# Weight conversion in a fused attention and two-MLP kernel: a leaky ReLU and two bit operations for a scaled copy and three, with the table of order keys laid anew

## The chip, the cores and the metric

The program runs on one core of one Trainium2 chip. The metric is the device time of one execution, in microseconds (us): the median of several runs. The engines are named as the profile names them: PE (TensorE matmuls; PEld its weight loads), DVE (VectorE), ACT (ScalarE), POOL (GpSimd), SP (SyncE, which only issues DMAs here).

## The reference

Linear attention with exponential features, then an MLP with SiLU, then an MLP with squared ReLU. 4 batches, 8 heads, 576 positions, head size 64, 128 features; 2304 tokens, model size 512, hidden size 2048.

```python
def phi(x):
    proj = np.einsum('bhsd,df->bhsf', x, w_phi)
    proj = proj - np.max(np.abs(proj), axis=-1, keepdims=True)
    return np.concatenate([np.exp(proj), np.exp(-proj)], axis=-1)
q_p, k_p = (phi(q), phi(k))
kv = np.einsum('bhsf,bhsd->bhfd', k_p, v)
z = np.sum(k_p, axis=2)
num = np.einsum('bhsf,bhfd->bhsd', q_p, kv)
den = np.einsum('bhsf,bhf->bhs', q_p, z)[..., None] + 1e-06
x = (num / den)                       # tokens x 512
h = x @ w_in                          # first MLP
x = (h * (1.0 / (1.0 + np.exp(-h)))) @ w_out
h = np.maximum(x @ w_in2, 0.0)        # second MLP
out = (h * h) @ w_out2
```

The weights of both MLPs reach the kernel as 64-bit floating-point numbers, read as pairs of 32-bit words. The kernel itself makes 32-bit numbers of them.

## The kernel before

Products in 32 bits are made of three passes: each operand is split into a high part (a rounding copy on ACT, `hi_act`, L446) and a low part (a subtraction, `lo_on`, L450, on DVE), and high times low, low times high and high times high are summed in PSUM. In the first batch's attention the products are taken on the 32-bit numbers directly.

Attention goes by batch and by pair of heads. `keys_of(j, p)` loads keys and values, projects (L856), takes the maximum (L861), subtracts it (L867) and takes exponentials of whole 512-column blocks (L948), or, for pairs from number `bx` on, lets ACT take them from PSUM in blocks of 128 columns with the maximum as a bias (L932, after a negation, L878); then it sums keys times values (`pkv`, L964). `queries_of(b, p)` does a block of 288 positions for a pair: projection `pq` (L1051), copy to `qp` (L1058), maximum over the partitions on POOL (`qm`, L1065), subtraction (L1071), two exponentials `qe` (L1083), numerator and denominator `pn` (L1117), copy to `qn` (L1120). The denominators go over memory: SP spreads them over 96 partitions (`rr`, L1134), DVE takes the reciprocal (L1137), SP stores it (L1140) and loads it back for 64 partitions (`qb`, L1143), DVE multiplies (x, L1159), and x is split into high and low part. In these names the first number is the batch or block, the second the pair; block b has the positions 288 b to 288 b + 287 of all tokens.

The first MLP (`chunk`) goes over six stretches of tokens and 16 chunks of 128 hidden units: `h` (L1198, 12 matmuls), its SiLU in four steps on ACT and DVE, and `o` (L1237). Its first `h` needs x of all four pairs of block 0, the fourth pair for the last three of the 12 matmuls. The second MLP takes seven products instead of eight over 2 x 2 blocks: sums of weights (`ws`, `ya`: `w_adds`, L684, on POOL), `pa`, `pb`, `pc` (L1366), and `y` (L1538).

Weights are converted by `w_conv`: `mag` on ACT multiplies the upper words, read as 32-bit numbers, by a power of two (`wc`, L560), and `bits` on DVE shifts left by three and clears the sign (L565), ors three bits of the lower word in (L569), and ors the sign in (L573). There are 16 of 1024 columns for the first MLP, in the attention of the first two blocks and the early chunks, and 32 of 512 columns for the second, later. `w_split` then makes the high and low part.

The order of all instructions is made ahead of time: every step is an `Op` with a key, an engine and a cost, and `Plan.run` plays the program through, gives each engine, whenever it is free, the ready step with the lowest key, and emits the steps in that order. Each engine then works through its own queue strictly in order, and SP its DMA issues likewise. The table `KEYS` holds the numbers that set the keys (and `bx`). Where the plan leaves PE idle over 1.9 us ahead of an attention product, `idle_mm` (L1683) puts filler matmuls there, one for about each 0.43 us.

Of the kernel before, what the change touches and what calls it, by code (L numbers as in the profile page):

```python
# [8 lines left out]
F32 = mybir.dt.float32  # L9
F32R = mybir.dt.float32r  # L10
I32 = mybir.dt.int32
AF = mybir.ActivationFunctionType
ALU = mybir.AluOpType
# [64 lines left out]
class Plan:  # L78
# [16 lines left out]
    def op(self, key, engine, cost, emit, r=(), w=(), bufs=(), unit=None, after=()):  # L95
        if unit and engine == "PE":
            key -= KEYS["pe"]
        elif unit:
            key -= KEYS["ee"] if unit.early else KEYS["e1"] if unit.soon else 0
        if not unit and engine in ("ACT", "DVE"):  # L100
            key -= KEYS["el"]
        o = Op(len(self.ops), key, engine, cost, emit, unit)
        before = set(after)
        for x in r:
            before.update(self.written[x])
        for x in w:
            before.update(self.read.pop(x, ()))
            before.update(self.written.get(x, ()))
        for x in r:
            self.read.setdefault(x, []).append(o)  # L110
        for x in w:
            self.written[x] = [o]
        if unit and unit.token:
            bufs = [*bufs, unit.token]
        for b in bufs:
            if b not in self.started:
                self.started.add(b)
                b.first = o
                o.allocs.append(b)
                if b.pool in self.last:  # L120
                    self.last[b.pool][0] += 1
            else:
                before.add(b.first)
            b.users += 1
            o.frees.append(b)
        before.discard(o)
        o.waits = len(before)
        for x in before:
            x.after.append(o)
        self.ops.append(o)  # L130
        if unit:
            unit.ops.append(o)
        return o
# [142 lines left out]
def dve(n, fast=False):  # L276
    return 70 + (0.52 if fast else 1.04) * n + 60
# [6 lines left out]
def dma(kb):  # L284
    return kb
# [3 lines left out]


KEYS = {
# [6 lines left out]
}  # L298


# [1 line left out]
def attention_then_two_mlps(ctx, tc, kT, qT, v, w_phi, w1, w2, out):  # L302
    nc = tc.nc
# [66 lines left out]
    op = plan.op  # L370
# [68 lines left out]
    def get(b):  # L439
        if b.tile is None:  # L440
            b.tile = b.make()
        return b.tile
# [95 lines left out]
    def w_conv(layer, c, parts, key):  # L538

        n = f"{layer}_{c}_{parts[0]}"
        cols = 512 * len(parts)
        u = plan.unit()
        if layer == 0:
            raw = w_tile("bits", c)
            f = Buf("raw", lambda: rp.tile([128, cols], F32, tag="raw", name="wc" + n), None)
        else:
            raw = Buf("raw", lambda: rp.tile([128, 2 * cols], I32, tag="raw", name="wr" + n), None)
            f = Buf("c", lambda: cp.tile([128, cols], F32, tag="c", name="wc" + n), None)  # L550

        def load():
            src = (w1, w2)[layer][c, :, parts[0] * 512:parts[0] * 512 + cols].bitcast(I32)
            nc.sync.dma_start(out=get(raw), in_=src)

        def halves():
            return get(raw).rearrange("p (n two) -> p n two", two=2)

        def mag():
            nc.scalar.activation(out=get(f), in_=halves()[:, :, 1].bitcast(F32), func=AF.Copy, scale=2.0 ** -112)  # L560

        def bits(i):
            b, lo, hi = get(f).bitcast(I32), halves()[:, :, 0], halves()[:, :, 1]
            if i == 0:
                nc.vector.tensor_scalar(  # L565
                    out=b, in0=b, scalar1=3, scalar2=0x7FFFFFFF, op0=ALU.logical_shift_left, op1=ALU.bitwise_and
                )
            elif i == 1:
                nc.vector.scalar_tensor_tensor(  # L569
                    out=b, in0=lo, scalar=29, in1=b, op0=ALU.logical_shift_right, op1=ALU.bitwise_or  # L570
                )
            else:
                nc.vector.scalar_tensor_tensor(  # L573
                    out=b, in0=hi, scalar=-(1 << 31), in1=b, op0=ALU.bitwise_and, op1=ALU.bitwise_or
                )

        k = ("wf", layer, c, parts[0])
        hold = max([0] + [NC * i + x for i in range(NL) for x in range(NC) if key_of(i, x) <= key - 6]) if layer else 0
        r = [(("c", 0, hold // NC, hold % NC), "h")] if layer else []
        ld = op(key - P["wl"], "SP", dma(cols), load, r=r, w=[(k, 0)], bufs=[raw])  # L580
        if layer == 0:
            ld.behind = splits.get(c - NWR)
        op(key, "ACT", act(cols) + cols / 10, mag, r=[(k, 0)], w=[(k, 1)], bufs=[raw, f], unit=u)
        for i in range(3):
            op(key, "DVE", dve(cols, i < 1), lambda i=i: bits(i), r=[(k, 1 + i)], w=[(k, 2 + i) if i < 2 else k],
               bufs=[raw, f], unit=u)
        return f, u

    def w_tile(layer, c, turn=0):
        if (layer, c, turn) not in wch:  # L590
            shape, dt = [128, 4, 512], F32R
            if layer in (1, 3) and c < 2:
                wch[layer, c, turn] = Buf(
                    "wl", lambda: wide_pool().tile([128, 8, 256], F32R, tag="w", bufs=2, name=f"wl{layer}_{c}"), None
                )
                return wch[layer, c, turn]
            if layer == "bits":
                shape, dt = [128, 2048], I32
            elif layer in (1, 3):
                shape = [128, 8, 256]  # L600
            first = c // 2 in (1, 2, 4, 6) if layer in (1, 3) else c in IN_W and not turn
            wch[layer, c, turn] = Buf(
                "w" if first else "wq",
                lambda: (wp if first else late_pool()).tile(
                    shape, dt, tag="w", bufs=NC - NW if first else NWQ, name=f"w{layer}_{c}_{turn}"
                ), None
            )
        return wch[layer, c, turn]
# [1049 lines left out]
    for i, (at, cols) in enumerate(BLOCKS):  # L1658
        for q in range(NQ):
            key = base3 + (NQ * i + q * cols / 512) * fine  # L1660
# [81 lines left out]
```

## Time and profile before

| what | us |
|---|---|
| median of 3 runs (lowest, highest) | 950.94 (949.41, 952.22) |
| span of the profiled execution, first to last instruction | 947.9 |
| PE busy | 939.2 |
| DVE busy | 723.2 |
| ACT busy | 608.8 |
| POOL busy | 149.3 |

The span is what the profile shows of one execution; the time of a run has some 3 us around it. Busy times are shares of the span; an engine that is not the bottleneck may idle at no cost. In the rows further below, a bracket or a number behind "idle before" is the time that the engine stood still just before, and the arrow names what ended that wait.

### The profile page before, as it was taken

Reading aid. Unit: us, or ns where it says so; the run is one execution under the profiler, and the core shown is the slowest. Engines: PE = TensorE matmul, PEld = TensorE weight load, DVE = VectorE, ACT = ScalarE, POOL = GpSimd, SP = SyncE. Lnnn points to the kernel's source line nnn. Section 1 sums busy time; section 2 is a strip of 40 time slices with the busy share of each in tenths; the row PEclk is TensorE's granted clock in tenths of the full one; section 3 lists DMA queues with packets and bytes.
Section 4 is the critical chain, followed back from the end, with each engine's and each line's share of the span. In section 5 each row is a group of like instructions: output and inputs, shape, how many; then the busy total and the mean of one; then the engine's idle time right before and its main releaser. Section 6 shows DMA issues by size and latency. Waiting matters only on the chain.

```text
span 947.9 us, 16861 instructions
## 1 busy us (share of the span) xinstructions
PE 939.2 (99%) x6142; PEld 908.8 (96%) x6142; DVE 723.2 (76%) x1229; ACT 608.8 (64%) x1358; POOL 149.3 (16%) x128
## 2 busy tenths in 40 slices
PE   9999999999999999999999999999999999999998
PEld 8769999999999999999999999999999999999998
DVE  6999998877667778989565876777466789887951
ACT  7989868888877787777334554666565665544431
POOL 3230013200022000321000333341101330000000
PEclk9999999999999999999999999999999999999999
DMA  8758634553324555667768775456336784543421
GB/s 325 251 195 278 224 147 153 175 161 107 121 77 134 191 180 188 207 181 228 232 230 288 256 272 179 160 206 205 116 130 233 226 290 142 156 149 119 145 81 66
DMA packets 83613, 175.44 MB, mean 185 GB/s; under 512 B 15050, under 2 KB 44874, under 8 KB 76874
## 3 DMA queue, kind: packets, MB, share of 16 engines
q1 hardware_dynamic: 83386, 174.23, 55.6%
q8 instruction: 48, 0.79, 0.3%
q14 instruction: 35, 0.29, 0.1%
q10 hardware_dynamic: 144, 0.13, 0.0%
HBM read 125.67 MB, written 48.59 MB: 184 GB/s over the span
## 4 chain that ended last, share of the span: by engine, by line
PE 92%; DVE 2%; ACT 1%; DMA 0%; issue 0%; POOL 0%; DVEq 0%; ACTq 0%
PE h L1198 21%; PE o L1237 21%; PE y L1538 19%; PE pb L1366 8%; PE pa L1366 5%; PE pc L1366 5%; PE pn L1117 4%; PE pkv L918 3%; PE pk L856 2%; PE pkv L964 2%; PE pq L1054 1%; PE pq L1055 1%; DVE w L450 0%; DVE x L1159 0%; ACT kp L932 0%; DVE qp L1071 0%
## 5 line engine op out<-in xcount | busy, mean ns | idle before, releaser
L1237 PE MATMUL o<-gh,w 128*128 128x432 f32 (+1 forms) x768 | 217.4, 340 | 0.0
L1198 PE MATMUL h<-x,w 128*128 128x432 f32 (+1 forms) x1152 | 216.1, 337 | 0.3 <-DVE w L450 0.3
L1198 PEld LDWEIGHTS h<-x,w 128*128 128x128 f32 x1152 | 195.9, 188 | 6.8 <-DVE w L450 0.5
L1237 PEld LDWEIGHTS o<-gh,w 128*128 128x128 f32 x768 | 139.9, 188 | 3.8
L1237 PE MATMUL o<-gl,w 128*128 128x432 f32 (+1 forms) x384 | 129.6, 338 | 0.0
L1065 POOL PARTITION_ALL_REDUCE qm<-qp x32 | 74.0, 2334 | 226.0 <-ACT qp L1058 212.4
L1202 ACT ACTIVATE a<-h 128x432 f32<-128x432 f32 (+1 forms) x96 | 47.4, 493 | 69.2 <-PE h L1198 69.0
L1206 DVE SCALAR_TENSOR_TENSOR a<-a,h 128x432 f32<-128x432 f32 (+1 forms) x96 | 52.8, 550 | 41.0 <-ACT a L1202 40.5
L1237 PEld LDWEIGHTS o<-gl,w 128*128 128x128 f32 x384 | 72.2, 188 | 1.9
L684 POOL TENSOR_TENSOR ws<-ws 128x256 f32<-128x256 f32 x52 | 45.8, 883 | 142.9 <-DVE w L450 108.4
L450 DVE TENSOR_TENSOR gl<-a,gh 128x432 fp32r<-128x432 f32 (+1 forms) x96 | 55.0, 572 | 15.3 <-ACT gh L446 14.5
L446 ACT CAST gh<-a 128x432 fp32r<-128x432 f32 (+1 forms) x96 | 49.9, 520 | 25.3 <-DVE a L1206 24.7
L890 ACT ACTIVATE ke<-pk,mx 112x128 f32<-112x128 f32 (+1 forms) x160 | 44.5, 374 | 0.0
L1083 ACT ACTIVATE qe<-qp 128x576 f32<-128x576 f32 x64 | 41.7, 682 | 4.2 <-DVE qp L1071 3.7
L1538 PE MATMUL y<-yb,w 128*128 128x256 f32 x316 | 44.0, 278 | 0.0
L450 DVE TENSOR_TENSOR qo<-qe,qh 128x576 fp32r<-128x576 f32 x48 | 38.7, 820 | 5.7 <-ACT qh L446 5.0
L1117 PE MATMUL pn<-qh,kv 128*65 128x288 f32 x192 | 42.9, 294 | 0.0
L1538 PEld LDWEIGHTS y<-yb,w 128*128 128x128 f32 x316 | 40.1, 188 | 0.0
L1381 DVE TENSOR_TENSOR glq<-pb,aq 128x384 f32<-128x384 f32 x24 | 13.3, 555 | 34.3 <-PE pb L1366 34.3
L964 PEld LDWEIGHTS pkv<-v,kp 112*128 112x128 f32 (+1 forms) x320 | 36.6, 192 | 0.3
L1159 DVE TENSOR_TENSOR x<-qn,qb 64x288 f32<-64x288 f32 x64 | 31.5, 492 | 7.1 <-DMA qb<-rd 6.6
L964 PE MATMUL pkv<-v,kp 112*128 112x128 f32 (+1 forms) x320 | 36.9, 275 | 0.0
(405 smaller groups left out, 2471.6 us busy)
## 6 DMA issues: line engine op xcount, KB each, us to landing
w<-w1d SPq DMA_DIRECT2D x30, 1024.0 KB, 5.3
wbits<-w SPq DMA_DIRECT2D x16, 1024.0 KB, 7.2
wr<-w SPq DMA_DIRECT2D x32, 512.0 KB, 5.3
fold<-gd SPq DMA_DIRECT2D x32, 512.0 KB, 3.7
w2d<-wc SPq DMA_DIRECT2D x32, 256.0 KB, 4.3
qr<-qT SPq DMA_DIRECT2D x56, 144.0 KB, 4.2
ws<-w2d SPq DMA_DIRECT2D x26, 256.0 KB, 4.0
w1d<-w SPq DMA_DIRECT2D x6, 1024.0 KB, 4.9
```

The source lines that it names most:

```text
L446: nc.scalar.copy(out=dst, in_=src)
L450: e.tensor_tensor(out=dst, in0=src, in1=hi.bitcast(F32), op=ALU.subtract)
L684: nc.gpsimd.tensor_tensor(out=get(f)[:, o], in0=get(f)[:, a], in1=get(f)[:, b], op=how)
L964: nc.tensor.matmul(get(ps)[:, o:o + 128], get(kps[2 * g + s])[:nt, 2 * i + a], get(vt)[:nt, c:c + 128], start=t == 0 and a == 0 and s == 0 ...
L1065: nc.gpsimd.partition_all_reduce(get(mx), get(pr).rearrange("p a t -> p (a t)"), 128, bass.bass_isa.ReduceOp.absmax)
L1117: nc.tensor.matmul(get(ps)[:D1, :HB], w, get(e)[:, t], start=x == 0, stop=x == len(ops) - 1)
L1198: nc.tensor.matmul(get(ps)[:, :cols], a, x[:, cc, :cols], start=k == 0, stop=k == 3 * ND - 1)
L1202: nc.scalar.activation(out=get(gb)[0][:, :cols], in_=get(ps)[:, :cols], func=AF.Tanh, scale=0.5)
L1206: nc.vector.scalar_tensor_tensor(out=a, in0=a, scalar=1.0, in1=get(ps)[:, :cols], op0=ALU.add, op1=ALU.mult)
L1237: nc.tensor.matmul(get(acc)[:, :cols], a, g[:, :cols], start=c == 0 and x == 0, stop=c == NC - 1 and x == 2)
L1366: nc.tensor.matmul(get(ps)[:, :QB], ws[a][:, f], row(b, y, cc), start=first and k == 0, stop=k == 5, skip_group_check=True,)
L1538: nc.tensor.matmul(get(acc)[:, d * 256:d * 256 + half], get(ws[a][0])[:, ws[a][1], s], both(y)[:, j], start=q == 0 and d == 0 and x == 0, ...
```

## The change

`mag` becomes a leaky ReLU (`Prelu`) with a scale of 2^16 and a slope of 2^-32 for negative numbers, so that the sign stays in place when the result is shifted left by three. The operation that set the sign, and the mask in the first one, go. So there are two bit operations for each conversion and not three. `Plan` is told of one step less. Nearly all numbers of `KEYS` change, `bx` from 3 to 4: the fourth pair of batch 0 takes its exponentials by 512 columns as well.

```diff
 KEYS = {
-    "k0s": 15.74, "q0s": 15.35, "q0": 6.0, "w0": 71.12, "ws": 0.43, "we": -9.35, "Q1": 57.33, "A1": -5.43,
+    "k0s": 17.1, "q0s": 15.35, "q0": 6.0, "w0": 71.19, "ws": 1.46, "we": -8.93, "Q1": 56.24, "A1": -4.91, "Q2":
...
         def mag():
-            nc.scalar.activation(out=get(f), in_=halves()[:, :, 1].bitcast(F32), func=AF.Copy, scale=2.0 ** -112)
+            nc.scalar.activation(
+                out=get(f), in_=halves()[:, :, 1].bitcast(F32), func=AF.Prelu, scale=2.0 ** 16, alpha=2.0 ** -32
+            )
 
         def bits(i):
-            b, lo, hi = get(f).bitcast(I32), halves()[:, :, 0], halves()[:, :, 1]
+            b = get(f).bitcast(I32)
             if i == 0:
-                nc.vector.tensor_scalar(
-                    out=b, in0=b, scalar1=3, scalar2=0x7FFFFFFF, op0=ALU.logical_shift_left, op1=ALU.bitwise_and
-                )
-            elif i == 1:
-                nc.vector.scalar_tensor_tensor(
-                    out=b, in0=lo, scalar=29, in1=b, op0=ALU.logical_shift_right, op1=ALU.bitwise_or
-                )
+                nc.vector.tensor_scalar(out=b, in0=b, scalar1=3, scalar2=None, op0=ALU.logical_shift_left)
             else:
                 nc.vector.scalar_tensor_tensor(
-                    out=b, in0=hi, scalar=-(1 << 31), in1=b, op0=ALU.bitwise_and, op1=ALU.bitwise_or
+                    out=b, in0=halves()[:, :, 0], scalar=29, in1=b, op0=ALU.logical_shift_right, op1=ALU.bitwise_or
                 )
...
-        for i in range(3):
-            op(key, "DVE", dve(cols, i < 1), lambda i=i: bits(i), r=[(k, 1 + i)], w=[(k, 2 + i) if i < 2 else k],
+        for i in range(2):
+            op(key, "DVE", dve(cols, i < 1), lambda i=i: bits(i), r=[(k, 1 + i)], w=[(k, 2) if i < 1 else k],
                bufs=[raw, f], unit=u)
```

The lines behind the diff stand four lower in the new file (L450 is the same line, L1159 becomes L1155). What the new numbers move is seen in the built order.

**SP ahead of the first h.** The DMA issues around the load of `qb0_3`, the reciprocals of block 0's fourth pair. Before:

```order
L1134 DMA rr0_3_592<-qn0_3_577 96x1x6
L1143 DMA qb0_2_612<-rd_98 64x576
L1140 DMA rd_98<-rr0_3_592 96x6
L1143 DMA qb0_3_651<-rd_98 64x576
L1134 DMA rr1_0_658<-qn1_0_640 96x1x6
L1134 DMA rr1_1_670<-qn1_1_660 96x1x6
L633 DMA w1d_96<-w0_4_0_642 128x2048
```

Now:

```order
L1130 DMA rr0_3_590<-qn0_3_575 96x1x6
L1139 DMA qb0_2_607<-rd_98 64x576
L1136 DMA rd_98<-rr0_3_590 96x6
L1130 DMA rr1_0_635<-qn1_0_623 96x1x6
L1130 DMA rr1_1_656<-qn1_1_645 96x1x6
L1139 DMA qb0_3_664<-rd_98 64x576
L629 DMA w1d_96<-w0_4_0_567 128x2048
```

The load of `qb0_3` has moved behind the two spreads of block 1's denominators.

**DVE at the same place**, up to the product x0_3 and what follows. `qp1` is the subtraction for block 1, `wc0` a conversion and `w0` a low part of the first MLP's weights. Before:

```order
L1137 RECIPROCAL rr0_3_592<-rr0_3_592 96x6
L573 SCALAR_TENSOR_TENSOR wc0_4_0_493<-wbits_4_0_371,wc0_4_0_493 128x1024
L1159 TENSOR_TENSOR x0_2_647<-qn0_2_501,qb0_2_612 64x288 x2
L1071 TENSOR_TENSOR qp1_2_596<-qp1_2_596,qm1_2_614 128x576
L1071 TENSOR_TENSOR qp1_3_607<-qp1_3_607,qm1_3_632 128x576
L450 TENSOR_TENSOR x_0_588<-x0_2_647,x_0_588 128x288
L450 TENSOR_TENSOR w0_4_0_642<-wc0_4_0_493,w0_4_0_642 128x2x512
L569 SCALAR_TENSOR_TENSOR wc0_5_0_547<-wbits_5_0_443,wc0_5_0_547 128x1024
L1159 TENSOR_TENSOR x0_3_688<-qn0_3_577,qb0_3_651 64x288 x2
L1137 RECIPROCAL rr1_0_658<-rr1_0_658 96x6
L573 SCALAR_TENSOR_TENSOR wc0_5_0_547<-wbits_5_0_443,wc0_5_0_547 128x1024
L450 TENSOR_TENSOR x_0_588<-x0_3_688,x_0_588 128x288
```

Now (the subtraction `qp1_2` and then the reciprocal `rr0_3` stand just ahead of these rows):

```order
L1067 TENSOR_TENSOR qp1_3_596<-qp1_3_596,qm1_3_605 128x576
L1155 TENSOR_TENSOR x0_2_637<-qn0_2_499,qb0_2_607 64x288 x2
L450 TENSOR_TENSOR w0_4_0_567<-wc0_4_0_451,w0_4_0_567 128x2x512
L450 TENSOR_TENSOR x_0_558<-x0_2_637,x_0_558 128x288
L450 TENSOR_TENSOR w0_5_0_577<-wc0_5_0_523,w0_5_0_577 128x2x512
L567 TENSOR_SCALAR wc0_6_0_538<-wc0_6_0_538 128x1024
L1133 RECIPROCAL rr1_0_635<-rr1_0_635 96x6
L569 SCALAR_TENSOR_TENSOR wc0_6_0_538<-wbits_6_0_472,wc0_6_0_538 128x1024
L1155 TENSOR_TENSOR x0_3_684<-qn0_3_575,qb0_3_664 64x288 x2
L1133 RECIPROCAL rr1_1_656<-rr1_1_656 96x6
L567 TENSOR_SCALAR wc0_7_0_669<-wc0_7_0_669 128x1024
L450 TENSOR_TENSOR x_0_558<-x0_3_684,x_0_558 128x288
```

The last bit operations on `wc0_4` and `wc0_5` are gone, and the low part of `w0_5` and work on `wc0_6` and `wc0_7` have moved ahead of the low part of x0_3; the reciprocal `rr0_3` has moved behind `qp1_2`.

**ACT around the copies to `qp1`**, which POOL's maxima of block 1 wait for. `qe0_3` are the last exponentials of block 0's queries, `wc0` conversions (L560), `w0` high parts, `kv0_3` the copy of keys times values, `qn` the copies of numerators and denominators. Before:

```order
L1083 ACTIVATE qe0_3_1_544<-qp0_3_481 128x576
L560 ACTIVATE wc0_5_0_547<-wbits_5_0_443 128x1024
L975 COPY kv0_3_554<-pkv0_3_503 128x260
L1058 COPY qp1_0_556<-pq1_0_0_549 128x288
L1058 COPY qp1_0_556<-pq1_0_1_552 128x288
L1058 COPY qp1_1_567<-pq1_1_0_558 128x288
L560 ACTIVATE wc0_6_0_569<-wbits_6_0_527 128x1024
L1120 ACTIVATE qn0_3_577<-pn0_3_0_562,eps_105 65x288
L1120 ACTIVATE qn0_3_577<-pn0_3_1_571,eps_105 65x288
L446 CAST x_0_588<-x0_0_574 128x288
L1058 COPY qp1_1_567<-pq1_1_1_579 128x288
```

Now (the first copy to `qp1_0` stands ahead of these rows):

```order
L1079 ACTIVATE qe0_3_1_535<-qp0_3_464 128x576
L560 ACTIVATE wc0_6_0_538<-wbits_6_0_472 128x1024
L1054 COPY qp1_0_479<-pq1_0_1_540 128x288
L971 COPY kv0_3_550<-pkv0_3_501 128x260
L1054 COPY qp1_1_554<-pq1_1_0_542 128x288
L446 CAST x_0_558<-x0_0_544 128x288
L1054 COPY qp1_1_554<-pq1_1_1_548 128x288
L1054 COPY qp1_2_564<-pq1_2_0_556 128x288
L446 CAST w0_4_0_567<-wc0_4_0_451 128x2x512
L1116 ACTIVATE qn0_3_575<-pn0_3_0_561,eps_105 65x288
L446 CAST w0_5_0_577<-wc0_5_0_523 128x2x512
L1054 COPY qp1_2_564<-pq1_2_1_579 128x288
```

The copies to `qp1_0` have moved ahead of `kv0_3`, and the high parts of `w0_4` and `w0_5` have moved ahead of the last copy to `qp1_2`.

Elsewhere: PE's filler rows ahead of the first h go from eight matmuls (16 passes, as a 32-bit product has two) at three places to two matmuls at one; the first 63 rows of PE and its last 2067 are the same; on ACT one conversion, one high part and one copy have moved ahead of the last copy to `qp0_3`. At the start of the second MLP DVE's low parts of the last `ws` and the first `ghq` stand in the same succession as before.

## Rows read from the trace of the kernel before

**Rows 1.** The page: busy us (share of the span) xinstructions; busy tenths.

```profile
PE 939.2 (99%) x6142; PEld 908.8 (96%) x6142; DVE 723.2 (76%) x1229; ACT 608.8 (64%) x1358; POOL 149.3 (16%) x128
```

**Rows 2.** Timeline, PE: start, us, engine, line, out<-in, count, idle before.

```profile
51.32 4.18 PE L1117 MATMUL pn<-qe,kv 128*65 128x288 f32 x16 [1.26 <-ACT qe L1083]
...
57.01 0.70 PE L1117 MATMUL pn<-qe,kv 128*65 128x288 f32 x2 [0.64 <-ACT qe L1083]
57.97 3.61 PE L1117 MATMUL pn<-qe,kv 128*65 128x288 f32 x14 [0.26 <-ACT qe L1083]
61.20 3.55 PE L1198 MATMUL h<-x,w 128*128 128x288 f32 x24
```

**Rows 3.** Timeline around the start of the second MLP, DVE, POOL and PE.

```profile
596.18 2.51 DVE L450 TENSOR_TENSOR w<-ws,w 128x256 fp32r<-128x256 f32 x4
...
596.73 3.36 POOL L684 TENSOR_TENSOR ws<-ws 128x256 f32<-128x256 f32 x4 [14.14 <-ACT g_0gh L1415]
...
599.21 0.44 PE L1366 MATMUL pb<-xt_5h,w 128*128 128x384 f32 x1 [0.93 <-DVE ghq L1381]
```

**Rows 4.** Groups by line and form, 24 to 62 us: busy us, mean ns.

```profile
L1683 PE MATMUL pn<-wbl 128*128 128x256 f32 x16 | 3.9, 379 | 0.0
```

**Rows 5.** Stretches: us, busy PE PEld DVE ACT POOL, PEclk, DMA share, GB/s.

```profile
50.00:55.00 5.00, 3.74 (x16) 2.04 (x16) 4.99 (x6) 3.90 (x7) 5.00 (x2) 1.00 0.10 27
```

**Rows 6.** Timeline, POOL, ahead of the first h.

```profile
44.39 2.65 POOL L1065 PARTITION_ALL_REDUCE qm<-qp  x1 [4.15 <-ACT qp L1058]
47.83 7.63 POOL L1065 PARTITION_ALL_REDUCE qm<-qp  x3 [0.78 <-ACT qp L1058]
```

**Rows 7.** Timeline, DVE, ahead of the first h.

```profile
52.18 0.18 DVE L1137 RECIPROCAL rr<-rr 96x6 f32<-96x6 f32 x1
...
55.42 1.43 DVE L1071 TENSOR_TENSOR qp<-qp,qm 128x576 f32<-128x576 f32 x2
...
57.13 1.22 DVE L450 TENSOR_TENSOR w<-wc,w 128x1024 fp32r<-128x1024 f32 x1
58.27 1.22 DVE L569 SCALAR_TENSOR_TENSOR wc<-wbits,wc 128x1024 int32<-128x1024 int32 x1
59.41 0.91 DVE L1159 TENSOR_TENSOR x<-qn,qb 64x288 f32<-64x288 f32 x2
...
61.55 0.45 DVE L450 TENSOR_TENSOR x<-x,x 128x288 fp32r<-128x288 f32 x1
...
62.02 1.25 DVE L565 TENSOR_SCALAR wc<-wc 128x1024 int32<-128x1024 int32 x2
```

**Rows 8.** Timeline, ACT, ahead of the first h.

```profile
31.51 2.17 ACT L932 ACTIVATE kp<-pk,mx 112x128 f32<-112x128 f32 x8
...
38.54 2.04 ACT L446 CAST w<-wc 128x1024 fp32r<-128x1024 f32 x2
41.13 1.26 ACT L1083 ACTIVATE qe<-qp 128x576 f32<-128x576 f32 x2 [0.55 <-DVE qp L1071]
42.30 1.15 ACT L560 ACTIVATE wc<-wbits 128x1024 f32<-128x1024 f32 x1
...
43.60 1.00 ACT L1058 COPY qp<-pq 128x288 f32<-128x288 f32 x3
...
57.24 1.81 ACT L1083 ACTIVATE qe<-qp 128x576 f32<-128x576 f32 x3
```

**Rows 9.** Timeline, SP's DMA issues, ahead of the first h.

```profile
53.83 0.44 SPq L1143 DMA_DIRECT2D qb<-rd  x1
55.36 2.55 SPq L1134 DMA_DIRECT2D rr<-qn  x2
```

**Rows 10.** Tile qb, 20 to 80 us: from issue to landing.

```profile
DMA to landing us min/median/max: 2.8/4.7/7.9
```

**Rows 11.** Groups by line and form: busy us, mean ns, idle before.

```profile
L573 DVE SCALAR_TENSOR_TENSOR wc<-wr,wc 128x512 int32<-128x512 int32 x32 | 21.9, 684 | 0.3
...
L573 DVE SCALAR_TENSOR_TENSOR wc<-wbits,wc 128x1024 int32<-128x1024 int32 x16 | 19.2, 1212 | 0.1
...
L948 ACT ACTIVATE kp<-kd 112x512 f32<-112x512 f32 x12 | 6.8, 633 | 4.5 <-DVE kd L867 4.5
```

10 rows, old and new, of the table KEYS are left out of this document.

## Prediction

> **What bounds the kernel now.** I read the page's busy times first: TensorE (PE) is busy 939.2 of 947.9 us, 99% of the span and in the tenths of every slice but the last, VectorE (DVE) 723.2, ScalarE (ACT) 608.8 [rows 1]. So PE bounds the kernel, and time can go only where PE stands still or works for nothing. The timeline of PE shows where that is. From the first matmul of the MLP, h at 61.20 [rows 2], it runs on, but for one longer wait of 0.93 us at 599.21 [rows 3]. Ahead of 61.20, in the attention of the first batch, it waits for `qe` before 51.32, 57.01 and 57.97, for 1.26, 0.64 and 0.26 us [rows 2], and runs 3.9 us of filler matmuls (L1683), 16 passes whose result is thrown away [rows 4]. Between 50 and 55 PE is busy 3.74 us of 5 and DVE 4.99 [rows 5]: there DVE is the full engine. The most that the early part can give back is fillers and waits, 3.9 + 2.2 = 6.1 us, 0.6% of the time.
>
> Two chains end at h. The first: the last of POOL's maxima ends at 47.83 + 7.63 = 55.46 [rows 6], DVE subtracts it (55.42 to 56.85 with its neighbour [rows 7]), ACT takes the exponentials (the last three end at 59.05 [rows 8]), PE multiplies until 61.20: 5.7 us from POOL's end to h. The second: the reciprocal `rr` of the fourth pair at 52.18 [rows 7], its store, the load of `qb` at 53.83 [rows 9], the product x at 59.41, its low part from 61.55 to 62.00 [rows 7]. That feeds the last quarter of h_0's 12 matmuls. The 24 matmuls of h_0 and h_1 take 3.55 us [rows 2], some 0.13 from start to start, so the eleventh is due at 62.5 and h_0 is through by 62.8. Both chains are within half a microsecond of deciding; shortening one alone gives little.
>
> **What is removed.** Sixteen bit operations of 1024 columns, 1.21 us each, and 32 of 512 columns, 0.68 us each [rows 11]: 19.2 + 21.9 = 41.1 us of DVE. Nearly all of it lies beside a full PE, which hides it, so it gives nothing by itself. Six of the sixteen stand ahead of the low part of x: 6 x 1.14 = 6.8 us of DVE (1.14 from start to start, as at 57.13, 58.27, 59.41 [rows 7]). The shift that loses its second scalar stays one instruction over the same data; I cost it as before, 0.62 (1.25 for two [rows 7]). The trace has no leaky ReLU. The nearest row is the exponential, 0.63 us for 512 columns [rows 11], against 1.15 for a conversion's 1024 [rows 8]: by columns they are alike, so I take no difference, with -0.1 and +0.1 us each as bounds, on an engine that is not the bound. The built program holds one table load, as before, so no switch of tables is added.
>
> **The first chain.** The fourth pair's keys go from narrow exponentials (eight take 2.17 us [rows 8], 20 some 5.4, with three negations 6.0) to four wide ones of 0.63 [rows 11] and two of half the width, some 3.3, and three DVE subtractions (512, 512 and 256 columns, by the 1.21 for 1024 some 0.6, 0.6, 0.3). That frees 2.7 us of ACT, but a conversion (1.15), a weight's high part (half of the 2.04 for two [rows 8]) and one copy (0.3), 2.5 us, now stand ahead of that pair's last copy. I take no shift. Behind `qe` (41.13 to 42.30) ACT now runs one conversion, 1.15, and then the copy, 0.3, that POOL's next maximum wants; before, `kv` and another copy were ahead of it. 42.30 + 1.15 + 0.3 = 43.7 against 44.3 (43.60 and two of three copies in 1.00 us [rows 8]): 0.6 us sooner, so POOL starts at 43.8 instead of 44.39. Its four maxima take 2.65 + 7.63 = 10.3 us [rows 6]. The 0.8 us that it waited between 47.04 and 47.83 can go, but the copy for the third now stands behind a weight's high part on ACT that waits for DVE, 0 to 1.2 us. With 0.4 of that POOL ends at 54.5 instead of 55.46 (54.1 to 55.3), and PE could start h at 60.2 instead of 61.20 (59.8 to 61.0).
>
> **The second chain.** Two things move against it. On DVE the `rr` of the fourth pair now stands behind the third subtraction, which needs POOL's third maximum; I put it near 54 instead of 52.18. On SP the load of `qb` now stands behind two spreads of the next block's denominators, which wait for ACT. Before, those two were issued from 55.36 to 57.91 [rows 9]; with the first chain some 0.7 us sooner the load goes out near 57.2 instead of 53.83. With the 2.8 us that such a load took at best [rows 10] it lands at 60.0. DVE has by then, from the fourth subtraction at 54.5: 0.72 (half of 1.43) + product 0.91 + weight 1.14 + x low part 0.45 + weight 1.14 + shift 0.62 + reciprocal 0.18 + or 1.14 = 6.3 [rows 7], so it turns to the product at 60.8 (before 59.41), and the load is not waited for. Then 0.91, a reciprocal 0.18 and a shift 0.62, and the low part (0.45) ends at 63.0, against 62.00. So although six operations are gone, those that are pulled ahead (a weight's low part, the shift and or of one weight, the shift of another) and the later `rr` fill their place. With the eleventh and twelfth matmul behind it h_0 is through near 63.2. The first chain alone would have it through 1.6 us after h starts, 60.2 + 1.6 = 61.8. My second sum counts the short operations at their full duration, not from start to start, and POOL at its middle, so it may be up to a microsecond long; I take 62.5 between the two, **-0.3 us** for the early part against 62.8, with bounds -1.5 (DVE's queue is short, the first chain decides and gains what it can) and +1.5 (every wait above at its upper end).
>
> **Later.** Between 62 and 590 us PE has no idle group of note before, and DVE only gets lighter. At 596.18 four low parts of weights on DVE take 2.51 us beside four POOL additions (from 596.73), and PE waits 0.93 us for the sum that stands behind them [rows 3]. In the new order DVE and POOL run the same operations there in the same succession, so I leave that wait in place: **0**, bounds -0.9 (DVE arrives early enough to have them done) and 0. PE's last 2067 rows are the same as before, the end too. New waits between 62 and 590: **0**, bounds 0 and +1.5.
>
> **Sum.** 947.9 - 0.3 + 0 + 0 = 947.6 us of span. The median of the runs is 3.0 us above the span of before, so 950.6 us (before 950.94). What a measurement of this kernel can tell from no change is about 0.3%, 2.9 us: faster is under 948.1, slower over 953.8.
>
> **Rivals.**
>
> (a) PE's early waits go: DVE, relieved of 6.8 us, comes to x in time and the first chain is shorter than my sum, so that h_0 is through 2.9 to 5 us sooner. For it: the fillers shrink from three places to one, 16 passes to 4, and their number follows what the planner expects PE to idle. Against: the queue of SP and the operations pulled ahead on DVE. With 3.5 us it is 950.94 - 3.5 = 947.4. Chance 0.22.
>
> (b) Slower: the load of `qb` on SP. It now waits for ACT's copies of the next block's denominators, and what stands behind it on SP waits too. If it lands 7.9 us after its issue, the longest of its kind [rows 10], x starts at 57.2 + 7.9 = 65.1 instead of 60.8, h_0 is through 2.4 us later (0.91 + 0.18 + 0.62 + 0.45 + 0.26), at 67.5 against 62.8, and the time is 950.94 + 4.7 = 955.6. Slower by 2.9 us it is when h_0 is through at 65.7, x begins at 63.3, and the landing takes 6.1 us. Against it: the median of such a landing is 4.7 [rows 10], and the DMA engines were busy a tenth of the time in 50 to 55 us [rows 5]. Chance 0.07.
>
> (c) The clock. In 50 to 55 us, with PE busy 3.74 of 5, the granted clock was 1.00, which is 2.4 GHz [rows 5]. With 4 filler passes PE does less there. If it were granted 1.2 GHz from there to h, 24 passes of `pn`, 0.26 us each (14 in 3.61 [rows 2]), would take 6.2 us more: 950.6 + 6.2 = 956.8 at most, as some is hidden behind the wait for x. The trace shows no fall at waits of up to 1.26 us and has no longer ones. Chance 0.05. The Trainium skill, page "TensorE: Matmul & The Clock Gate", section "HAM oscillation — how this bites in real kernels", says that gaps in which PE idles bring the clock back to half rate; by it the fillers would be worth their time and the sum would be that of this rival, by the row it is that of the forecast.
>
> (d) The new order of the middle (keys and queries of the later batches, the second layer's weights) costs PE 3 to 4 us of new waits: 953.6 to 954.6. Against it: DVE loses work there. Chance 0.05.
>
> The forecast, h_0 through within 1.5 us of 62.5 and no more than 1.5 us of new waits behind it, has chance 0.61.
>
> **How the numbers follow.** Forecast 950.6. Its own bounds are 950.6 - 1.5 - 0.9 = 948.2 and 950.6 + 1.5 + 1.5 = 953.6; (a) reaches below, (b) to (d) above. To leave out no more than 2 in 10 the range goes to 946.8, which holds most of (a), and to 954.0. Faster by over 0.3%: (a), 0.22. Slower: (b), (c) and a little of (d), 0.13. Within: 0.65.
>
> **What would show it.** Right: DVE some 40 us less busy and PE's span all but the same; h's first matmul sooner than 61.2, but a pause within the first twelve until x's low part ends near 63; `qb` of the fourth pair issued near 57; the wait for `ghq` near 599 still there. Wrong: x's low part before 61 (then (a)), `qb` landing after 63 (b), a granted clock under 1.00 before h (c), PE waits between 62 and 590 (d), or conversions on ACT that take over 1.3 us.

## The result and the profile after

The changed kernel took 959.06 us (median; 958.54 to 960.83), beside 951.13 for the kernel before: a ratio of 1.009, interval 1.0074 to 1.0107. It is 0.9% slower, 8 us. The prediction was 950.6, within 946.8 to 954.0; the time lies 5 us above that range.

The page's busy times of the changed kernel, as in [rows 1]; its span is 957.1 us, 9.2 more than before. (In the runs that are listed with their spans, a run's time lies 1.7 to 2.1 us above its span, not 3. So the 947.9 of before belongs to an execution some 1.3 us faster than the median, and the difference of the spans is that much more than the difference of the medians.)

```profile
PE 940.5 (98%) x6130; PEld 907.2 (95%) x6130; DVE 688.0 (72%) x1184; ACT 607.2 (63%) x1341; POOL 150.8 (16%) x128
```

VectorE (DVE) has 35.2 us less to do. TensorE (PE) is as busy as before, and the span grew all the same: PE stands still more. The view of waits says where; its columns are who waited for whom, us in sum, times, and the longest. PE from 62 to 940 us, the kernel before:

```profile
PE pb L1366 <- DVE ghq L1381: 0.9, 1, 0.9
PE h L1198 <- DVE w L450: 0.3, 1, 0.3
```

The changed kernel:

```profile
PE pb L1362 <- DVE glq L1377: 3.1, 1, 3.1
PE pq L1050 <- DVE ql L450: 1.7, 2, 1.2
PE h L1194 <- ACT x L446: 0.7, 1, 0.7
PE o L1233 <- ACT gh L446: 0.6, 1, 0.6
PE o L1233 <- DVE gl L450: 0.4, 2, 0.2
PE pq L1050 <- ACT qn L1116: 0.4, 1, 0.4
PE pb L1362 <- DVE ghq L1377: 0.4, 1, 0.4
```

Two kinds of wait have become ten, of which seven are shown. The same can be counted from PE's starts: the distance from one matmul's start to the next, less the regular distance for its shape (0.12 us for 256 columns, 0.13 for 288, 0.17 for 384, 0.20 for 432), summed over a stretch. In this table "before" has its stretches at the same work, where that lies some us earlier.

| stretch of the changed kernel, us | lost before | lost now | difference |
|---|---|---|---|
| start of h (61.20 before, 60.57 now) | | | -0.63 |
| from h to 70, without the keys' products | 0.40 | 2.32 | +1.92 |
| 70 to 160 | 4.64 | 5.07 | +0.43 |
| 160 to 210 | 0.08 | 1.84 | +1.76 |
| 210 to 400 | 0.59 | 0.54 | -0.05 |
| 400 to 445 | 0 | 3.45 | +3.45 |
| 590 to 612 | 1.29 | 0.65 | -0.63 |
| 612 to 640 | 0 | 3.35 | +3.35 |
| behind 640 | 0.46 | 0.06 | -0.41 |

The differences add up to the 9.2 us of span. (Of what is lost between 70 and 160 in both kernels, some 2 us lie in the keys' products, part of which stand further apart than the regular distance.) The early part cost 1.3 us net. The rest is 7.9 net: three places that the prediction had put at nought make up 8.6, and small gains take some of it back.

The table sets one execution against one. Three runs further below stand in the order of the changed kernel up to 330 us at least (the old pace, `xs` on VectorE, stores reckoned late). In them h starts at 59.50, 60.27 and 59.55, the early part costs 0.2, 0.8 and 0.3 us net, and the stretch from 160 to 210 loses 1.44, 0.08 and 1.16. So the first rows, and place 3 below, hold to about a microsecond.

**Place 1, 612 us.** DVE, POOL and PE in the changed kernel, from the timeline (start, us, engine, line, operation, count, idle before and what ended it):

```profile
612.05 6.60 DVE L450 TENSOR_TENSOR w<-ws,w 128x256 fp32r<-128x256 f32 x4
618.58 0.54 DVE L1377 TENSOR_TENSOR glq<-pb,aq 128x384 f32<-128x384 f32 x1
...
609.61 4.83 POOL L1314 TENSOR_TENSOR xs<-xr 128x768 f32<-128x768 f32 x2
614.41 3.96 POOL L1314 TENSOR_TENSOR xs<-xr,xs 128x768 f32<-128x768 f32 x2
...
619.18 0.44 PE L1362 MATMUL pb<-xt_3h,w 128*128 128x384 f32 x1 [3.09 <-DVE glq L1377]
```

The kernel before, the same four low parts, and the same four additions on POOL:

```profile
606.44 1.41 DVE L450 TENSOR_TENSOR w<-ws,w 128x256 fp32r<-128x256 f32 x4
...
630.75 3.98 POOL L1318 TENSOR_TENSOR xs<-xr 128x768 f32<-128x768 f32 x2
634.70 4.57 POOL L1318 TENSOR_TENSOR xs<-xr,xs 128x768 f32<-128x768 f32 x2
```

Four low parts that took 1.41 us take 6.60 when POOL's wide additions (`xs`) run beside them, and the sum `glq` that PE waits for stands behind them. Before, `xs` began 24 us behind these four low parts: in POOL's queue it stood behind the sums `ya5` and `ya7`, which had to wait for DVE. In the new order these two come ahead of the last `ws`, so nothing holds `xs` back.

**Place 2, 416 to 440 us.** ACT's queue, from the timeline of the changed kernel:

```profile
416.31 0.66 ACT L560 ACTIVATE wc<-wr 128x512 f32<-128x512 f32 x1 [3.58 <-DMA w2d<-wc]
...
430.78 0.67 ACT L560 ACTIVATE wc<-wr 128x512 f32<-128x512 f32 x1 [5.19 <-DMA w2d<-wc]
...
433.12 0.54 ACT L446 CAST gh<-a 128x432 fp32r<-128x432 f32 x1
```

ACT stands at a conversion that needs a buffer, and the buffer is free only when the store of the weights before the last has landed. Behind the conversion on ACT wait the SiLU and the high part `gh`, and PE waits for that at 433.72. Over the whole program, the group of these conversions (busy us, mean ns, idle before it and what ended that), before and now:

```profile
L560 ACT ACTIVATE wc<-wr 128x512 f32<-128x512 f32 x32 | 21.4, 674 | 10.2 <-DMA wr<-w 8.2 <-DMA w2d<-wc 1.1 <-DMA ws<-w2d 0.9
```

```profile
L560 ACT ACTIVATE wc<-wr 128x512 f32<-128x512 f32 x32 | 21.5, 673 | 24.8 <-DMA w2d<-wc 23.5 <-DMA wr<-w 1.1
```

23.5 us of waiting for stores in place of 1.1. Two keys stand behind this: `w2a` 66.15 to 66.29 and `w2b`, the step from one conversion to the next, 1.8 to 0.72. The 32 conversions now lie between 333 and 487 us; before they lay between 336 and 567. There are two buffers, and a store takes 5.8 us in the median from issue to landing. The leaky ReLU itself costs nothing: 673 ns against 674.

**Place 3, 166 us.** DVE in the changed kernel:

```profile
159.36 1.92 DVE L1155 TENSOR_TENSOR x<-qn,qb 64x288 f32<-64x288 f32 x2 [1.34 <-DMA qb<-rd]
161.31 0.19 DVE L1133 RECIPROCAL rr<-rr 96x6 f32<-96x6 f32 x1
...
165.12 0.91 DVE L1155 TENSOR_TENSOR x<-qn,qb 64x288 f32<-64x288 f32 x2 [1.49 <-DMA qb<-rd]
166.07 0.76 DVE L450 TENSOR_TENSOR ql<-qr,ql 64x576 fp32r<-64x576 f32 x1
```

A product x that takes 0.91 us took 1.92, since POOL's maximum began at 159.40. So the reciprocal behind it, its store and its load came a microsecond later, DVE stood 1.49 us for that load, and `ql`, which PE needs, stood behind.

### The profile page after: what moved, and what is told of

Read it like the earlier page. It is cut to its first block, busy times and chain, and to the rows that moved or that the text cites. A ratio compares the mean times of both kernels' runs of the same rounds, so it can differ in the third digit from the quotient of the medians.

```text
span 957.1 us, 16766 instructions
## 1 busy us (share of the span) xinstructions
PE 940.5 (98%) x6130; PEld 907.2 (95%) x6130; DVE 688.0 (72%) x1184; ACT 607.2 (63%) x1341; POOL 150.8 (16%) x128
## 4 chain that ended last, share of the span: by engine, by line
PE 83%; DMA 6%; DVE 6%; ACT 3%; issue 1%; POOL 1%; SPq 0%; DVEq 0%; ACTq 0%
PE y L1534 19%; PE o L1233 18%; PE h L1194 17%; PE pb L1362 7%; PE pc L1362 5%; PE pa L1362 5%; PE pk L852 3%; PE pkv L914 3%; PE pkv L960 3%; DMA w2d<-wc 2%; PE pn L1113 2%; DMA wbits<-w 2%; DVE w L450 1%; DMA qb<-rd 1%; DVE x L1155 1%
## 5 line engine op out<-in xcount | busy, mean ns | idle before, releaser
L450 DVE TENSOR_TENSOR gl<-a,gh 128x432 fp32r<-128x432 f32 (+1 forms) x96 | 62.4, 650 | 20.4 <-ACT gh L446 19.9
L680 POOL TENSOR_TENSOR ws<-ws 128x256 f32<-128x256 f32 x52 | 49.3, 950 | 158.9 <-DVE w L450 110.0
L1155 DVE TENSOR_TENSOR x<-qn,qb 64x288 f32<-64x288 f32 x64 | 33.5, 523 | 13.2 <-DMA qb<-rd 12.7
L450 DVE TENSOR_TENSOR w<-ws,w 128x256 fp32r<-128x256 f32 (+2 forms) x39 | 34.3, 907 | 11.3 <-ACT w L446 7.4
L450 DVE TENSOR_TENSOR qo<-qe,qh 128x576 fp32r<-128x576 f32 x48 | 35.1, 750 | 6.2 <-ACT qh L446 3.4
L560 ACT ACTIVATE wc<-wr 128x512 f32<-128x512 f32 x32 | 21.5, 673 | 24.8 <-DMA w2d<-wc 23.5
```

The costliest lines, as they stand in the source:

```text
L450: e.tensor_tensor(out=dst, in0=src, in1=hi.bitcast(F32), op=ALU.subtract)
L680: nc.gpsimd.tensor_tensor(out=get(f)[:, o], in0=get(f)[:, a], in1=get(f)[:, b], op=how)
```

## What the experiments showed

Three theories stood at the start. A, **the pace**: the time is lost through the keys `w2a` and `w2b`, at places 1 and 2. B, **the operations**: the new conversion itself costs it. C, **the early part**: fillers and the load of `qb` ahead of h. Where an experiment changes a key or an operation, the plan is played anew and other instructions move too, unless the text says otherwise.

**The new conversion with all keys of before.** All 32 numbers that the change sets go back, among them

```diff
-    "w2a": 66.29, "w2b": 0.72, "bx": 4,
+    "w2a": 66.15, "w2b": 1.8, "bx": 3,
```

> The changed kernel with every key of the table as before (bx = 3 too): the leaky ReLU and the two bit operations alone. Theory A (the pace): the 8 us come from one key, the step from one conversion of the second MLP's weights to the next (w2b, 1.8 before, 0.72 now), so this kernel is within 2 us of before, 949 to 953, with under 0.5 us of PE's waits between 400 and 450 us and no wait over 1.2 us near 600 to 620. Theory B (the operations): the conversion itself costs the time, by a slower ScalarE instruction or by what a lighter VectorE triggers: 957 to 960.

965.24 us, ratio 1.0151 (1.0137 to 1.0164). Neither theory said that much. With the old pace the conversions no longer wait for stores; their idle time is all for loads:

```profile
L560 ACT ACTIVATE wc<-wr 128x512 f32<-128x512 f32 x32 | 21.6, 675 | 13.3 <-DMA wr<-w 13.3
```

But ahead of h PE stands 4.48 us at once for `qe`, after which the granted clock is 0.50 from 52 to 56 us; and between 400 and 450 PE loses some 7 us where theory A had left under 0.5: there ACT stands in line 3.68 us for a load of weights and 2.88 for a load of queries. So the stores behaved as theory A said, and its time failed: old numbers played with one operation less are a new order too, and a bad one.

**The old conversion with all new keys.** The same 32 numbers, set in the kernel before:

```diff
-    "w2a": 66.15, "w2b": 1.8, "bx": 3,
+    "w2a": 66.29, "w2b": 0.72, "bx": 4,
```

> The kernel before, with three bit operations and the scaled copy, and the new table of keys (bx = 4 too). Theory A (the pace): as slow as the changed kernel or slower, 957 to 962, since a converted buffer is held by one operation more; ScalarE waits over 15 us in sum for the stores of converted weights (1.1 us before). Theory B (the operations): 949 to 953.

969.08 us, ratio 1.0192 (1.0176 to 1.0209). Slow as A said, and slower than its 957 to 962. ACT waits for the stores, as it said:

```profile
L560 ACT ACTIVATE wc<-wr 128x512 f32<-128x512 f32 x32 | 21.3, 669 | 29.1 <-DMA w2d<-wc 29.0
```

Yet only some 5 of the 18 us are lost between 400 and 450; the rest goes in many waits of up to 1.7 us elsewhere. These two runs cannot price the conversion. They show that neither half of the change stands by itself: a table of keys is made for one set of operations.

**The changed kernel with the old pace.**

```diff
-    "w2a": 66.29, "w2b": 0.72,
+    "w2a": 66.15, "w2b": 1.8,
```

> The changed kernel with the two keys of the second MLP's weights (start w2a and step w2b) as before, all others new. In its order POOL's sums ya5 and ya7 stand behind the last ws again. Theory A (the pace): both the waits between 416 and 440 us (3.4 us) and the one at 619 us (3.3 us) go: 959.1 - 6.7 = 952.4, between 951.3 and 954. Theory B (the operations) or a cause ahead of 62 us (the load of qb): 957 to 960.

953.34 us, ratio 1.0027 (1.0016 to 1.0038): 5.7 us of the loss are gone with two keys. ACT no longer waits for stores, `xs` stands behind `ya5` and `ya7` again, and the four low parts take 1.42 us:

```profile
609.05 1.42 DVE L450 TENSOR_TENSOR w<-ws,w 128x256 fp32r<-128x256 f32 x4
...
633.37 3.98 POOL L1314 TENSOR_TENSOR xs<-xr 128x768 f32<-128x768 f32 x2
```

It is at the upper end of what A said, since 1.2 us of waits are left between 400 and 450 (PE stands 0.81 for `gl` at 446).

**Place 1 alone: POOL's wide additions on VectorE.**

```diff
-            e = "DVE" if s == 0 else "POOL"
+            e = "DVE"
```

> The changed kernel with the eight additions of 768 columns for the later blocks of the second MLP (xs, L1314) on VectorE and not on POOL, all keys new. If POOL's four additions beside VectorE's low parts are what makes four of them take 6.6 us at 612 us, these take about 1.4 us again and PE's wait of 3.25 us at 619 goes: 959.1 - 3.2 = 955.9 (955 to 957). If the low parts are slow for another reason, or VectorE is late there anyway, the wait stays or moves: 958 to 960.

953.95 us, ratio 1.0038 (1.0025 to 1.0051). All of the program up to 590 us stands in the order of the changed kernel. DVE at the place:

```profile
609.16 1.42 DVE L450 TENSOR_TENSOR w<-ws,w 128x256 fp32r<-128x256 f32 x4
611.17 0.56 DVE L1377 TENSOR_TENSOR glq<-pb,aq 128x384 f32<-128x384 f32 x1 [0.59 <-PE pb L1362]
```

Now DVE waits for PE and not PE for DVE: the wait of 3.1 us is gone, and POOL beside DVE was its cause. The gain, 5.1 us, is more than the 3.2 expected. The profiled execution shows where the rest may lie, in unchanged order: the stretch of place 3 loses 0.08 us and not 1.84, and place 2 some 0.8 less. At place 3 the product came 0.75 us sooner, ahead of POOL's maximum at 159.15:

```profile
158.61 0.92 DVE L1155 TENSOR_TENSOR x<-qn,qb 64x288 f32<-64x288 f32 x2 [0.84 <-DMA qb<-rd]
```

0.92 us, and PE did not wait at 165. So what place 3 costs hangs on a few tenths of a microsecond; that POOL's maximum is its cause is read from these two traces, and no run moves it alone.

**Place 2 alone: the plan is told when stores land.**

```diff
-        op(key, "SP", dma(256), store, r=[k], w=[(k, "d")], bufs=[f], unit=u)
+        op(key, "SP", dma(256), store, r=[k], w=[(k, "d")], bufs=[f], unit=u).late = 3500
```

> The changed kernel with all its keys, but the plan reckons 3.5 us more until a stored half of converted weights has landed (the plan puts 3.0 us, the trace shows 5.8 in the median, up to 9.6), so that it starts fewer conversions whose buffer isn't free yet. If ScalarE's wait in line for these stores is what starves TensorE between 416 and 440 us, ScalarE's waits for them fall from 23.5 us to under 8 and TensorE's waits between 400 and 450 from 3.45 to under 1.5. POOL's sums ya5 and ya7 stand behind the last ws in its order, so the wait at 619 goes too: 952 to 954. If the waits of 416 to 440 come from VectorE or from loads, they stay: 955 to 957.

953.60 us, ratio 1.0033 (1.0022 to 1.0044), with the new pace of 0.72 kept. The conversions' waits:

```profile
L560 ACT ACTIVATE wc<-wr 128x512 f32<-128x512 f32 x32 | 21.4, 673 | 1.8 <-DMA wr<-w 1.7
```

No wait for a store is left, PE loses 1.1 us between 400 and 450 where it lost 3.45, and place 1 is gone with it, by the order. That is the cause below the key: the plan reckons that a store has landed 3.0 us after its issue, the chip takes 5.8, and ACT pays the difference in line.

**The new pace alone, in the kernel before.**

```diff
-    "w2a": 66.15, "w2b": 1.8,
+    "w2a": 66.29, "w2b": 0.72,
```

> The kernel before, three bit operations and its own keys, with the start and step of the second MLP's weights alone as in the changed kernel (w2a 66.29, w2b 0.72). The pace theory: ScalarE waits over 15 us for the stores (1.1 before) and TensorE 2 to 8 us between 350 and 500 us: 953 to 960. ya5 and ya7 stay behind the last ws, so there is no wait over 1.5 us between 600 and 640. If the pace only harms together with the new operations or the other keys: 949.5 to 952.

956.36 us, ratio 1.0062 (1.0047 to 1.0077). ACT waits 29.6 us for stores and PE loses 5.1 us between 400 and 450 (none before), with three bit operations and old keys otherwise. So place 2 needs neither the new conversion nor the rest of the table.

**The early part: the reciprocal and x of block 0 first**, on top of the old pace.

```diff
-        op(key, "SP", dma(3), spread, r=[(Q, "num", 0), (Q, "num", 1)], w=[(Q, "r0")], bufs=[num, rr], unit=u).late = 1500
+        op(key, "SP", dma(3), spread, r=[(Q, "num", 0), (Q, "num", 1)], w=[(Q, "r0")], bufs=[num, rr], unit=u).late = 1500 if b else 0
...
-        op(key, "DVE", 2 * dve(HB), mul, r=[(Q, "r3"), (Q, "num", 0), (Q, "num", 1), *ahead], w=[(Q, "x")],
+        op(key - 40 * (b == 0), "DVE", 2 * dve(HB), mul, r=[(Q, "r3"), (Q, "num", 0), (Q, "num", 1), *ahead], w=[(Q, "x")],
```

> As the run with w2a and w2b of before (953.3), and in block 0 the plan reckons no extra 1.5 us for a spread of denominators and puts the product x first: the reciprocal rr0_3 stands ahead of VectorE's subtraction qp1_2, the load of qb0_3 ahead of the second spread of block 1, and fewer weight operations ahead of x's low part. If the second chain (rr, qb, x's low part) is what holds the first h, its waits between 61 and 70 us (2.0 us, before 0.4) fall under 0.8 and the time to 951 to 952.3. If the first chain or something else holds it, 952.8 to 954.

968.46 us, ratio 1.0189 (1.0164 to 1.0214). h_0 and h_1 run without a pause, 0.4 us lost from h to 70 as before, but hardly because x came sooner: its low part starts at 61.91, against 62.19 in the run with the old pace, on which this one builds. h itself starts at 61.57 and not at 59.50 as there, and the product behind h_1 at 64.97 and not at 64.63. So this run doesn't show which chain holds the first h; that the second one does (rr, `qb`, x) rests on PE's two waits for x in the trace of the changed kernel, shown in the next section. And a few instructions moved ahead of h played out into another program behind: no fillers at all ahead of h, and waits of 2.7 us for x at 245 and 3.9 for `gh` at 455. The forecast of the whole from one place failed, as mine had.

**The conversion alone, order kept.** Here the plan goes on reckoning with a third bit operation that issues nothing, so that all engines' instructions stand as before and only DVE's third operation is gone. In the kernel before, the leaky ReLU takes the place of the copy, the shift loses its mask, and

```diff
-            else:
-                nc.vector.scalar_tensor_tensor(
-                    out=b, in0=hi, scalar=-(1 << 31), in1=b, op0=ALU.bitwise_and, op1=ALU.bitwise_or
-                )
```

> The leaky ReLU and the two bit operations in the order of the kernel before: the plan still reckons with a third bit operation, which issues nothing, so every engine's instructions stand as before and VectorE's third bit operation is gone. This is the conversion alone, which the run with the old keys was not, since the plan was played anew there. If the order costs the time and the conversion nothing: 948.5 to 951.5, TensorE's waits as before (1.3 us near 599, none over 0.6 elsewhere behind 62 us), ScalarE's conversions 0.67 and 1.15 to 1.19 us each. If the conversion costs by itself: over 953.

949.58 us, ratio 0.9989 (0.9980 to 0.9999) to the kernel before: 0.6 us faster by the medians, with an interval that ends just short of 1: the one version here that beats both kernels. PE ahead of h:

```profile
57.49 3.61 PE L1117 MATMUL pn<-qe,kv 128*65 128x288 f32 x14 [0.26 <-ACT qe L1083]
60.72 3.55 PE L1198 MATMUL h<-x,w 128*128 128x288 f32 x24
```

h starts 0.48 us sooner than in [rows 2] and runs through. That is of the size of the gain, but one execution can't show that it is the gain: in the run with the new pace alone, whose order is that of the kernel before up to 360 us, h starts at 61.97, 0.77 later than in [rows 2]. 34.9 us of DVE less are worth half a microsecond or so, since PE covers the rest. Theory B is out.

**The order alone, conversion undone.** The old conversion in the order of the changed kernel: the third bit operation follows the second at once, and nothing else moves. In the changed kernel the copy takes the place of the leaky ReLU, the shift has its mask again, and the second step is

```diff
+            for x, n, o in ((lo, 29, ALU.logical_shift_right), (hi, -(1 << 31), ALU.bitwise_and)):
+                nc.vector.scalar_tensor_tensor(out=b, in0=x, scalar=n, in1=b, op0=o, op1=ALU.bitwise_or)
```

> The scaled copy and three bit operations in the order of the changed kernel: the second bit operation is followed at once by the third, all other instructions stand as in the changed kernel. If the order costs the time, this one is as slow as the changed kernel or slower (its buffers are held 0.7 us longer each): 958 to 964, with the waits near 420 to 440 and 619 us. If the conversion costs the time: 950 to 953.

975.92 us, ratio 1.0276 (1.0259 to 1.0293), more than I had thought. The waits for stores (20.3 us) and the one at place 1 are there:

```profile
627.08 6.61 DVE L450 TENSOR_TENSOR w<-ws,w 128x256 fp32r<-128x256 f32 x4
...
634.21 0.69 PE L1362 MATMUL pb<-xt_3h,w 128*128 128x384 f32 x1 [3.10 <-DVE glq L1377]
```

With the runs that keep an order, the four corners are:

| | order of before | new order |
|---|---|---|
| scaled copy, three bit operations | 950 to 951 | 975.9 |
| leaky ReLU, two bit operations | 949.6 | 959.1 |

The conversion gains 0.6 us in the old order and 17 in the new one, which leans on it. The largest part of the 17, 5.8 us, lies ahead of h: with the old conversion DVE is busy 5.82 of 6 us from 44 to 50 (4.86 in the changed kernel), PE stands 3.16 us ahead of 47.34 and 3.46 ahead of 56.65, the granted clock is 0.50 behind each (48 to 50 and 58 to 60 us), and h starts at 66.40 and not at 60.57. The order costs 9.5 us where the conversion is the new one.

**The fillers**, taken out of the run with the order kept. All 16 passes go, 12 of them between 48 and 56 us and four near 35.

```diff
-                    idle_mm(o.allocs[0], int((o.start - end - 900) / 430))
+                    pass
```

> The run with the conversion in the order of before (949.6), without the filler matmuls (12 passes, in stretches that end before h). Everything else stands as there. If the fillers only take up time in which TensorE waits anyway, the time stays at 949 to 950.5 and the granted clock at 1.00 up to h. If they keep the clock: a wait of about 3.1 us (1.24 and the 1.9 of the fillers) ahead of the products pn near 51 us is followed by a granted clock under 1.00, up to 16 passes of 0.13 us more each, and the time is 950.5 to 953.

950.08 us, ratio 0.9995 (0.9985 to 1.0005), some 0.5 us over the run with them; the intervals overlap. In the trace the effect is plain. PE, and the stretches (us, busy of PE, PEld, DVE, ACT and POOL, granted clock, DMA share, GB/s):

```profile
51.66 5.60 PE L1117 MATMUL pn<-qe,kv 128*65 128x288 f32 x16 [2.99 <-ACT qe L1083]
```

```profile
50.00:52.00 2.00, 0.34 (x1) 0.29 (x2) 2.00 (x3) 1.07 (x2) 2.00 (x2) 0.83 0.27 74
52.00:54.00 2.00, 2.00 (x5) 0.91 (x4) 1.99 (x4) 1.49 (x4) 2.00 (x2) 0.50 0.03 1
```

After a wait of 2.99 us the granted clock is 0.50, that is 1.2 GHz, and sixteen products take 5.60 us that took 4.18 [rows 2]. h starts at 61.70, 0.98 us later than with fillers; 0.41 of that was there ahead of the place already (the products of `pn` at 44.09 in place of 43.68), so the 12 passes may be worth some 0.6 us of the 1.42, and the rest hides in the waits for `qe` that follow. Executions of one order differ in h's start by as much, so this price is not shown.

## Why the prediction was wrong

**What bounds the kernel:** right. PE's standing still is all that changed the time; 35 us of DVE did not.

**What is removed:** right. The conversions on ACT cost what they did, and the run with the order kept puts the gain at 0.6 us. (DVE is 35.2 us less busy, not 41.1: operations overlap their neighbours, 1.22 long and 1.14 from start to start, and 1.75 came in with three more subtractions of the keys.)

**The first chain:** close in its end, by luck in part, since its terms were off in both directions. POOL began 1.1 us later than the sum had it (44.91 for 43.8): ACT stood for a load at the conversion ahead of the copy, a wait that the sum had at nothing. Its four maxima took 9.24 us, without any gap, for 10.3 and a gap of 0.4; they ended at 54.15 (54.5). From there to h it took 6.4 us (5.7), and h started at 60.57 (60.2).

```profile
43.40 1.13 ACT L560 ACTIVATE wc<-wbits 128x1024 f32<-128x1024 f32 x1 [1.15 <-DMA wbits<-w]
...
44.91 9.24 POOL L1061 PARTITION_ALL_REDUCE qm<-qp  x4 [4.90 <-ACT qp L1054]
```

**The second chain:** the working was right, the choice behind it was not. The load of `qb` was issued at 58.28 (57.2), the product started at 61.35 (60.8), and the low part started at 62.97 and ended at 63.4 (63.0). PE shows the pause within the first h, 0.75 us for the high part of x, which the sum did not have, and 0.19 for the low part:

```profile
60.57 1.56 PE L1194 MATMUL h<-x,w 128*128 128x288 f32 x9
62.89 0.40 PE L1194 MATMUL h<-x,w 128*128 128x288 f32 x1 [0.75 <-ACT x L446]
63.47 2.10 PE L1194 MATMUL h<-x,w 128*128 128x288 f32 x14 [0.19 <-DVE x L450]
```

I then took 62.5 as a middle between this chain and the first, where the later of the two decides. The sum alone (63.2) would have said +0.4. With h's start, the net up to 70 us was 1.3 against the -0.3 forecast, inside the bound of 1.5.

**Later, near 599:** right as far as it went: the wait for `ghq` is still there, 0.38 in place of 0.93. But I looked at that place alone. POOL's `xs` came forward onto the next four low parts, 10 us on. The rows of POOL's order show it: with `ya5` and `ya7` ahead of the last `ws`, the next in its queue is `xs`. The bound was 0; it was +3.35. So this term failed as well.

**New waits between 62 and 590: 0, bounds 0 and +1.5.** This is the step that failed first. It measured 5.6 us (1.8 at 160 to 210, 3.45 at 400 to 445, some tenths ahead of them). Rival (d) named 3 to 4 us of new waits, and got 0.05, because "DVE loses work there". At place 2 DVE's load had no part in it: the wait came from ACT, which stands in line for a buffer that a store holds. At place 3 DVE came late in spite of less work, behind a product slowed beside POOL's maximum and a load. I had read how closely the second layer's conversions now follow each other only as DVE's relief, and had not asked which resource sets how fast they may follow: two buffers and the landing of a store.

**Rivals:** (a) did not come, (b) neither: the load of `qb` was issued at 58.28, and DVE went from its queue to the product at 61.35 without waiting. (c) did not come in the changed kernel: the granted clock stayed at 1.00 up to h with 4 filler passes. In the runs where PE stood 2.7 us and more there it fell, so 0.05 was low for its kind, but not for this kernel.

## What to carry to other kernels

A change that speeds an engine nobody waits for gains little (0.6 us here), while a new order played out for it can cost far more (9.5 us). So keep the order fixed when you want to price an operation, and price the order as a change of its own. When steps follow each other more closely, look for what each of them holds until a DMA has landed, and which in-order queue waits for it. When work on POOL loses what held it back, look at what DVE does at its new time.

## What the runs showed of the hardware

**POOL beside DVE.** Between 612.66 and 618.58 us DVE did three low parts of 256 columns, 5.9 us, while POOL did additions of 768 columns, 2.0 us each from start to start; alone four take 1.41. So DVE got one such operation done for each of POOL's. With POOL's additions of 256 columns (0.8 us) the four took 2.51 [rows 3]. The Trainium skill, page "SBUF — State Buffer", section "🔬 SBUF: two separate sides", says that the two engines share a port pair under an exclusive lock, held for a whole instruction, which a VectorE operation with two inputs in SBUF needs beside a GpSimd one that reads SBUF. The additions agree with that. The maxima don't hold DVE so long: beside one of 2.41 us the product x took 1.92 where it takes 0.91, one microsecond more.

**The clock.** Waits of PE of nearly the same length were followed by different clocks. In the run with the reciprocal first PE stood 2.69 us ahead of 50.33 and then got 0.50:

```profile
48.00:50.00 2.00, 0.00 (x0) 0.00 (x0) 2.00 (x3) 0.88 (x3) 1.42 (x1) 1.00 0.17 59
50.00:52.00 2.00, 1.20 (x3) 0.49 (x4) 2.00 (x3) 2.00 (x6) 1.35 (x1) 0.72 0.07 16
52.00:54.00 2.00, 2.00 (x6) 0.98 (x5) 1.68 (x4) 1.56 (x4) 2.00 (x2) 0.50 0.00 0
```

In the changed kernel PE stood 3.09 us ahead of 619.18, and the clock stayed:

```profile
616.00:620.00 4.00, 0.91 (x6) 0.82 (x6) 3.93 (x5) 0.51 (x1) 2.29 (x2) 1.00 0.14 49
620.00:624.00 4.00, 4.00 (x25) 4.00 (x24) 1.80 (x4) 1.99 (x4) 0.00 (x0) 1.00 0.13 49
```

So a wait of about 3 us may cost itself alone or a stretch at half speed behind it; which one, the runs don't settle.
